# Retention and two feed-forward layers: decay tables for the queries, and another start order of weights and first steps

## The chip, the cores and the metric

One core of one Trainium2 chip. The metric is device time in microseconds (us), the median of three runs: 961.13 us before (960.35 to 962.30). Below, PE is TensorE, ACT is ScalarE, DVE is VectorE, POOL is GpSimd and SP is the queue that issues the transfers.

## What is computed

Four sequences of 576 positions, 8 heads of 64 columns. Attention without a softmax: the scores are scaled and multiplied by a decay, one gamma for each head. Its output (2304 tokens of 512) goes through two feed-forward layers, all in float32.

```python
gamma = 1.0 - 2.0 ** (-5.0 - np.arange(H))
Dmat = np.where(rel >= 0, gamma[:, None, None] ** rel[None, :, :], 0.0)
attn = np.matmul(scores * Dmat, v)              # scores = q k^T / sqrt(64)
h = x @ w_in                                    # x: 2304 x 512, w_in: 512 x 2048
x2 = (np.maximum(h, 0) + alpha * np.minimum(h, 0)) @ w_out
y = (sigmoid(x2 @ w_gate) * (x2 @ w_val)) @ w_out2   # d_ff 1536
```

## The kernel before, in words

The 2304 tokens are cut into blocks of 256, 512, 512, 512 and 512 (`BLOCKS`, line 27); block 0 is the short one. Attention goes by chunks of at most 128 positions (`CHUNKS`), 21 in all: two of block 0, five of block 1 (one of them of 64 positions, and another at its end), the rest of blocks 2 to 4.

Attention in chunks. For a chunk, q is multiplied by gamma to the power of the position inside the chunk and k (through v's rows) by its inverse, both on POOL (`att_q`, line 252, and `att_v`, line 260). PE makes the scores s (`att_scores`, line 267), DVE masks them, and PE makes o from the masked scores and v (`att_values`, line 285). What earlier chunks of the sequence give stands in a state `m_sb`, one 128x128 block for each pair of heads: PE multiplies it with q into o (line 294), then makes the chunk's own k-v product m (line 300), DVE adds it into the state (line 308, or copies it for a first chunk, line 310), and POOL multiplies the whole state by gamma to the power of the chunk's length (line 313), so that it fits the next chunk. The next chunk's product with the state waits for that. `split` (line 125) leaves the result as two float32r parts, the high one by ACT, the rest by DVE; the two parts of x and of each weight are multiplied in three products (`products`, line 384), which stand for one float32 product.

The weights come as raw words of 512 KB and are made into two such parts in `prepare_weight` (line 143): two ACT passes (lines 149 and 151), three DVE steps (155, 156, 159), one ACT pass (166) and one last DVE step (168). `begin_weight` starts one and issues the load of a further one; `weight_step(n)` (line 204) adds n to a credit, begins a weight whenever the credit reaches 1, and moves all that are under way by one step. `weight(...)` does so until a weight that is asked for is there. The first layer has 32 such blocks: key (1, f, 0) is a column block of w_in, (1, f, 1) a row block of w_out, f from 0 to 15.

`ffn1_h(j, f)` (line 393) makes hidden block f of token block j: 12 matmuls, then ACT and DVE apply the two slopes (lines 400 to 405), then the split into g. The two PSUM buffers of `ps_h` are free again after g's split on DVE (line 128). `ffn1_y(j, f)` (line 418) adds g times w_out's block into four output accumulators.

The order of PE's work is the program's own (a manual schedule). On the other engines a scheduler sets the order of the instructions when the program is built, and each engine's queue runs in that order. The program starts with `att_run` (line 349) over the seven chunks of blocks 0 and 1, whose argument `pace` says how fast weights are prepared beside it (`PACE_A`, `PACE_B`), and whose `fill` puts `EARLY` hidden blocks of token block 0 between the chunks, from chunk `LATE` on. Then a loop over f (line 501) makes the rest of block 0, with `BESIDE` = 11 of block 1's 16 steps beside it. The loop over token blocks 1 to 4 (line 519) has the attention of the block behind it as stages between its steps (`att_stages`, line 335), and prepares the second layer's weights in block 4; the second layer closes.

All weights, raw words, chunks (qk, kv) and g lie in one pool `big` of `NSLOT` = 39 slots of 4 KB a partition (line 92). A load waits until a slot is free.

Of the kernel before, what the change touches and what calls it, by code (L numbers as in the profile page):

```python
# [26 lines left out]
BLOCKS = (256, 512, 512, 512, 512)  # L27
FIRST = tuple(sum(BLOCKS[:j]) for j in range(len(BLOCKS)))
NBLK = len(BLOCKS)
NSLOT = 39  # L30

ORDER = (1, 2, 3, 4, 0)

NEXTRA = 1


EARLY, LATE = 5, 2

BESIDE = 11

# [2 lines left out]
BEHIND = 2  # L43


PACE_A, PACE_B, PACE_C, PACE_E, PACE_F = 0.55, 0.5, 0.7, 0.65, 1


def chunks():
# [12 lines left out]


CHUNKS = chunks()


LENGTHS = sorted({c[3] for c in CHUNKS})
O_M = NPAIR * P
O_GK = O_M + P
O_GP = O_GK + H  # L70
N_CST = O_GP + len(LENGTHS) * NPAIR


def constants():
    gamma = (1.0 - 2.0 ** (-5.0 - np.arange(H, dtype=np.float32))).astype(np.float64)
    i = np.arange(P)
    head = 2 * np.arange(NPAIR)[None, :] + (i // D)[:, None]
    out = np.zeros((P, N_CST), np.float32)
    out[:, :O_M] = (gamma[head][:, :, None] ** i / np.sqrt(D)).reshape(P, -1)
    out[:, O_M:O_GK] = i[None, :] >= i[:, None]  # L80
    out[:, O_GK:O_GP] = gamma ** -i[:, None]
    out[:, O_GP:] = (gamma[head][:, None, :] ** np.array(LENGTHS)[None, :, None]).reshape(P, -1)
    return out


# [1 line left out]
def retention_two_ffn(ctx: ExitStack, tc: tile.TileContext, att, cst, alpha, w1, w2, out):  # L87
# [85 lines left out]

    to_load = [(1, f, 0) for f in range(EARLY)]
    for f in range(NF1):
        to_load += [(1, f + EARLY, 0)] * (f + EARLY < NF1) + [(1, f, 1)]
    to_prepare = list(to_load)
    under_way = []

# [40 lines left out]
    def load_chunk(n):  # L220
        if n >= len(CHUNKS) or n in raw_a:
            return
        load_qk(n)
        load_kv(n)
# [27 lines left out]
    x_t = {}  # L252
    def att_q(n):

        c = CHUNKS[n][3]
        for part in (slice(0, 2), slice(2, 4)) if n == 0 else (slice(0, 4),):
            q = raw_a[n][0][:, 0, part, :c]
            nc.gpsimd.tensor_tensor(out=q, in0=q, in1=decay[:, part, :c], op=ALU.mult)  # L258

    def att_v(n):  # L260

        c = CHUNKS[n][3]
        v = raw_a[n][1][:c, 1, :].rearrange("p (h d) -> p h d", h=H)
        gk = c_sb[:c, O_GK:O_GP]
        nc.gpsimd.tensor_tensor(out=v, in0=v, in1=gk.unsqueeze(2).to_broadcast([c, H, D]), op=ALU.mult)

    def att_scores(n, pool, tags):
# [17 lines left out]
    def att_values(n, s_sb, pool, tags):  # L285

        j, _, pos, c, col = CHUNKS[n]
        qk, kv = raw_a[n]
        last = pos + c == S
        o_ps = pool.tile([P, NPAIR, P], F32, tag=tags[0], name=f"o{n}")  # L290

        if pos:
            for pr in range(NPAIR):
                nc.tensor.matmul(o_ps[:, pr, :c], m_sb[:, pr, :], qk[:, 0, pr, :c], start=pr == 0, stop=False)  # L294
        if not last:
            m_ps = pool.tile([P, NPAIR, D], F32, tag=tags[1], name=f"m{n}")
            for pr in range(NPAIR):
                for e in range(2):
                    h = 2 * pr + e
                    nc.tensor.matmul(  # L300
                        m_ps[e * D:(e + 1) * D, pr, :], kv[:c, 0, h * D:(h + 1) * D],
                        kv[:c, 1, h * D:(h + 1) * D], start=True, stop=True,
                    )
            for e in range(2):
                r = slice(e * D, (e + 1) * D)
                dst = m_sb[r, :, e * D:(e + 1) * D]
                if pos:
                    nc.vector.tensor_tensor(out=dst, in0=dst, in1=m_ps[r], op=ALU.add)
                else:
                    nc.vector.tensor_copy(dst, m_ps[r])  # L310
            g = O_GP + LENGTHS.index(c) * NPAIR
            g = c_sb[:, g:g + NPAIR].unsqueeze(2).to_broadcast([P, NPAIR, P])
            nc.gpsimd.tensor_tensor(out=m_sb, in0=m_sb, in1=g, op=ALU.mult)
        for pr in range(NPAIR):
            for e in range(2):
                h = 2 * pr + e
                nc.tensor.matmul(  # L317
                    o_ps[e * D:(e + 1) * D, pr, :c], kv[:c, 1, h * D:(h + 1) * D], s_sb[e][:c, pr, :c],
                    start=pos == 0 and pr == 0, stop=pr == NPAIR - 1,
                )  # L320
        x = x_t[j]
        split(x[:, 0, :, col:col + c], x[:, 1, :, col:col + c], o_ps[:, :, :c])
# [147 lines left out]
    nc.gpsimd.memset(m_sb, 0.0)  # L470
    load_chunk(0)
    load_chunk(1)
    load_weights(1)
    load_chunk(2)
    nc.sync.dma_start(out=al_sb, in_=alpha)
    nc.scalar.activation(na_sb, al_sb, AF.Copy, scale=-1.0)
    load_weights(2)
    load_chunk(3)
    load_weights(1)

    pa, py = (ps_a, "ab"), (ps_y, "yy")
    n0, n1 = len(runs_of(0)), len(runs_of(1))
# [14 lines left out]

    att_run(runs_of(0) + runs_of(1), [pa, py, py], lambda i: PACE_A if i < n0 else PACE_B, first_h, 4)

    step1 = 0  # L500
    for f in range(NF1):
        if done[0] < NF1:
            ffn1_h(0, done[0])
            done[0] += 1
            weight_step(PACE_C)
        ffn1_y(0, f)
        weight_step(PACE_C)
        if step1 * NF1 < BESIDE * (f + 1):
            ffn1_h(1, step1)
            weight_step(PACE_C)  # L510
            later(BEHIND - 1)
            weight_step(PACE_C)
            late.append((1, step1))
            step1 += 1
    n = runs_of(2)[0]
    load_chunk(n)
    att_q(n)
# [89 lines left out]
```

## Time and profile before

| | |
|---|---|
| Median of three runs | 961.13 us |
| The profiled execution | 963.9 us, its span 962.0 us |
| PE busy | 925.9 us, 96% of the span |
| PE weight loads | 777.5 us (beside PE) |
| DVE busy | 441.1 us, 46% |
| ACT busy | 288.8 us, 30% |
| POOL busy | 64.9 us, 7% |
| Moved by the transfers | 69.8 MB, 73 GB/s in the mean |

The span is the time from the first to the last instruction of one profiled execution. Busy times of different engines overlap. Shares of the whole span are means over stretches with different limits, so they are to be read with the views by stretch. A wait is idle time of an engine, put down to the instruction that ended it.

### The profile page before, as it was taken

How to read it: one execution, taken by the hardware profiler on the slowest of the kernel's cores; microseconds unless marked ns; L12 is line 12 of the kernel's file. 1: busy time of each engine (PE TensorE's matmuls, PEld its weight loads, DVE VectorE, ACT ScalarE, POOL GpSimd, SP SyncE). 2: the span in 40 equal slices, each digit the busy share in tenths (PEclk: the TensorE clock that was granted, in tenths of full speed). 3: DMA queues.
4: the chain of work that ended last, by engine and by line, in shares of the span. 5: the costliest groups of instructions: out<-in, count | busy, mean ns of one | idle time of the engine just before them, and what ended most of it. 6: DMA issues, size and time to landing. Idle time of an engine off the chain costs nothing.

```text
span 962.0 us, 12270 instructions
## 1 busy us (share of the span) xinstructions
PE 925.9 (96%) x5032; PEld 777.5 (81%) x5032; DVE 441.1 (46%) x730; ACT 288.8 (30%) x532; POOL 64.9 (7%) x62
## 2 busy tenths in 40 slices
PE   5777999999999999999999999999999999999998
PEld 4666998888888888887888888888888888888897
DVE  4999952545444544449877851221122112211212
ACT  2577820111011101137766641121112111211211
POOL 5410000131120111000000000000000000000000
PEclk9868999999999999999999999999999999999999
DMA  9932201332110310035552500100011000100100
GB/s 326 382 116 79 76 2 44 110 110 88 45 44 24 100 53 23 22 114 195 154 165 101 192 22 1 65 24 1 0 48 41 1 1 33 33 1 1 44 1 22
DMA packets 27975, 69.81 MB, mean 73 GB/s; under 512 B 6928, under 2 KB 8464, under 8 KB 27920
## 3 DMA queue, kind: packets, MB, share of 16 engines
q1 hardware_dynamic: 27920, 69.04, 21.2%
q8 instruction: 39, 0.64, 0.3%
q14 instruction: 16, 0.13, 0.0%
HBM read 59.59 MB, written 9.44 MB: 72 GB/s over the span
## 4 chain that ended last, share of the span: by engine, by line
PE 89%; DVE 7%; issue 1%; DMA 1%; ACT 1%; SPq 0%; DVEq 0%; ACTq 0%
PE z L388 31%; PE h L388 19%; PE y L388 18%; PE o L388 15%; DVE r L156 2%; DVE r L159 1%; PE s L275 1%; PE o L317 1%; DVE w L168 1%; PE o L294 1%; PE y0b L388 1%; PE y0a L388 1%; DMA r<-w 1%; DVE t L155 1%; PE m L300 1%
## 5 line engine op out<-in xcount | busy, mean ns | idle before, releaser
L388 PE MATMUL z<-x,w 128*128 128x512 f32 (+1 forms) x1440 | 305.3, 368 | 0.0
L388 PEld LDWEIGHTS z<-x,w 128*128 128x128 f32 x1440 | 252.4, 188 | 45.9
L388 PE MATMUL h<-x,w 128*128 128x512 f32 (+1 forms) x960 | 220.1, 380 | 11.6 <-DVE g L128 11.2
L388 PEld LDWEIGHTS h<-x,w 128*128 128x128 f32 x960 | 172.0, 195 | 46.3 <-DVE g L128 14.0
L388 PE MATMUL y<-g,w 128*128 128x512 f32 x768 | 187.5, 393 | 1.9 <-ACT yst L415 1.9
L388 PEld LDWEIGHTS y<-g,w 128*128 128x128 f32 x768 | 143.9, 189 | 33.7 <-ACT yst L415 2.3
L455 DVE TENSOR_TENSOR z<-sg,z 128x512 f32<-128x512 f32 (+1 forms) x60 | 38.6, 643 | 258.2 <-PE z L388 258.2
L388 PE MATMUL o<-w,p 128*128 128x512 f32 x648 | 156.8, 389 | 0.0
L388 PEld LDWEIGHTS o<-w,p 128*128 128x128 f32 x648 | 120.9, 188 | 24.6
L127 ACT ACTIVATE g<-h 128x512 fp32r<-128x512 f32 (+1 forms) x80 | 44.2, 553 | 232.7 <-DVE h L405 222.7
L404 DVE TENSOR_SCALAR t<-h,al_sb 128x512 f32<-128x512 f32 (+1 forms) x47 | 34.5, 734 | 113.2 <-PE h L388 113.2
L454 ACT ACTIVATE sg<-z 128x512 f32<-128x512 f32 (+1 forms) x60 | 33.3, 554 | 170.8 <-PE z L388 170.7
L127 ACT ACTIVATE p<-z 128x512 fp32r<-128x512 f32 (+1 forms) x60 | 33.4, 556 | 131.8 <-DVE z L455 131.8
L128 DVE TENSOR_TENSOR g<-h,g 128x512 fp32r<-128x512 f32 (+1 forms) x80 | 50.8, 634 | 25.6 <-ACT g L127 25.0
L128 DVE TENSOR_TENSOR p<-z,p 128x512 fp32r<-128x512 f32 (+1 forms) x60 | 38.2, 637 | 32.6 <-ACT p L127 32.5
L156 DVE CUSTOM_DVE_ANT_0 r<-r,t 128x1024 uint16<-128x1024 uint16 x68 | 49.3, 729 | 4.1 <-ACT r L151 0.2
L159 DVE SCALAR_TENSOR_TENSOR r<-r 128x512 uint32<-128x512 uint32 x68 | 49.9, 734 | 0.5
L149 ACT ACTIVATE r<-r 128x512 f32<-128x512 f32 x68 | 45.5, 669 | 12.0 <-DMA r<-w 12.0
L166 ACT ACTIVATE w<-r 128x512 fp32r<-128x512 f32 x68 | 44.0, 672 | 15.9 <-DVE r L159 14.8
L168 DVE TENSOR_TENSOR w<-r,w 128x512 fp32r<-128x512 f32 x68 | 46.3, 698 | 1.6 <-ACT w L166 1.5
L151 ACT ACTIVATE r<-r 128x512 int32<-128x512 uint32 x68 | 45.9, 675 | 0.0
L258 POOL TENSOR_TENSOR qk<-qk,c_sb 128x512 f32<-128x512 f32 (+1 forms) x21 | 25.0, 1193 | 160.1 <-DMA qk<-att 160.1
(45 smaller groups left out, 510.8 us busy)
## 6 DMA issues: line engine op xcount, KB each, us to landing
r<-w SPq DMA_DIRECT2D x68, 512.0 KB, 4.4
kv<-att SPq DMA_DIRECT2D x16, 512.0 KB, 4.1
qk<-att SPq DMA_DIRECT2D x15, 512.0 KB, 3.5
y<-ost SPq DMA_DIRECT2D x18, 256.0 KB, 2.0
x2d<-yst SPq DMA_DIRECT2D x16, 256.0 KB, 2.1
x2r<-x2d SPq DMA_DIRECT2D x16, 256.0 KB, 2.9
qk<-att SPq DMA_DIRECT2D x6, 256.0 KB, 3.7
kv<-att SPq DMA_DIRECT2D x4, 256.0 KB, 6.3
```

Source lines behind the costliest of these rows:

```text
L127: nc.scalar.activation(hi, src, AF.Copy)
L128: nc.vector.tensor_tensor(out=lo, in0=src, in1=hi.bitcast(F32), op=ALU.subtract)
L149: nc.scalar.activation(high.bitcast(F32), high.bitcast(F32), AF.Copy, scale=2.0 ** -112)
L151: nc.scalar.activation(low.bitcast(I32), low, AF.Copy, scale=2.0 ** -29)
L156: nc.vector.tensor_tensor(out=low.bitcast(I32), in0=low.bitcast(I32), in1=top.bitcast(I32), op=ALU.add)
L159: nc.vector.scalar_tensor_tensor(low, high, 0x80000000, low, ALU.bitwise_and, ALU.bitwise_or)
L166: nc.scalar.activation(w[:, 0, :], low.bitcast(F32), AF.Copy)
L168: nc.vector.tensor_tensor(out=w[:, 1, :], in0=low.bitcast(F32), in1=w[:, 0, :].bitcast(F32), op=ALU.subtract)
L388: nc.tensor.matmul(ps, l, r, start=first and i == 0, stop=last and i == len(todo) - 1)
L404: nc.vector.tensor_scalar(t, ps, 0.0, al_sb[:, f:f + 1], ALU.min, ALU.mult)
L454: nc.scalar.activation(t, ps[0], AF.Sigmoid)
L455: nc.vector.tensor_tensor(out=ps[1], in0=t, in1=ps[1], op=ALU.mult)
```

## The change

q's decay table of a chunk that isn't the first of its sequence is no longer the table of positions inside the chunk: ACT multiplies that table by gamma to the power of the chunk's start, in four pieces of up to 128 columns, into a tile `dec` of two buffers, and POOL multiplies q by it. v gets the inverse power of the position in the sequence. The state is then the plain sum of the chunks' products, and POOL's multiplication of it is gone. The constants hold the inverse powers and the factors for the five starts (748 columns where there were 656). The pool has 38 slots.

The start has another order as well. Loads: chunk 2 now comes ahead of the first weight, and chunk 3 ahead of the second. In the list of weights (1, f, 1) comes ahead of (1, f + EARLY, 0), and `EARLY` is 2 instead of 5. Fewer weights are prepared beside attention (`PACE_A` 0.08 for 0.55, `PACE_B` 0.14 for 0.5), two hidden blocks of block 0 stand between its chunks instead of five, and the loop over f takes block 1's step ahead of block 0's, with two of block 1's hidden blocks at its very start.

```diff
-NSLOT = 39
+NSLOT = 38
...
-EARLY, LATE = 5, 2
+EARLY, LATE = 2, 4
...
-PACE_A, PACE_B, PACE_C, PACE_E, PACE_F = 0.55, 0.5, 0.7, 0.65, 1
+PACE_A, PACE_B, PACE_C, PACE_E, PACE_F = 0.08, 0.14, 0.5, 0.65, 1
...
-        to_load += [(1, f + EARLY, 0)] * (f + EARLY < NF1) + [(1, f, 1)]
+        to_load += [(1, f, 1)] + [(1, f + EARLY, 0)] * (f + EARLY < NF1)
...
     def att_q(n):
 
-        c = CHUNKS[n][3]
+        _, _, pos, c, _ = CHUNKS[n]
+        by = decay
+        if pos:
+
+            by = ap.tile([P, NPAIR, P], F32, tag="dec", name=f"dec{n}", bufs=2)
+            for pr in range(NPAIR):
+                g = O_GP + STARTS.index(pos) * NPAIR + pr
+                nc.scalar.activation(by[:, pr, :c], decay[:, pr, :c], AF.Copy, scale=c_sb[:, g:g + 1])
         for part in (slice(0, 2), slice(2, 4)) if n == 0 else (slice(0, 4),):
             q = raw_a[n][0][:, 0, part, :c]
-            nc.gpsimd.tensor_tensor(out=q, in0=q, in1=decay[:, part, :c], op=ALU.mult)
+            nc.gpsimd.tensor_tensor(out=q, in0=q, in1=by[:, part, :c], op=ALU.mult)
...
                     nc.vector.tensor_copy(dst, m_ps[r])
-            g = O_GP + LENGTHS.index(c) * NPAIR
-            g = c_sb[:, g:g + NPAIR].unsqueeze(2).to_broadcast([P, NPAIR, P])
-            nc.gpsimd.tensor_tensor(out=m_sb, in0=m_sb, in1=g, op=ALU.mult)
...
     load_chunk(1)
+    load_chunk(2)
     load_weights(1)
-    load_chunk(2)
+    load_chunk(3)
     nc.sync.dma_start(out=al_sb, in_=alpha)
     nc.scalar.activation(na_sb, al_sb, AF.Copy, scale=-1.0)
     load_weights(2)
-    load_chunk(3)
-    load_weights(1)
...
+    load_weights(2)
     step1 = 0
     for f in range(NF1):
+
+        while step1 < EARLY or (step1 - EARLY) * (NF1 - 1) < (BESIDE - EARLY) * f:
+            ffn1_h(1, step1)
+            weight_step(PACE_C)
+            later(BEHIND - 1 if step1 >= EARLY else EARLY)
+            late.append((1, step1))
+            step1 += 1
+            if step1 > EARLY:
+                break
+        ffn1_y(0, f)
+        weight_step(PACE_C)
+        weight_step(PACE_C)
         if done[0] < NF1:
             ffn1_h(0, done[0])
             done[0] += 1
-            weight_step(PACE_C)
-        ffn1_y(0, f)
         weight_step(PACE_C)
-        if step1 * NF1 < BESIDE * (f + 1):
-            ffn1_h(1, step1)
-            weight_step(PACE_C)
-            later(BEHIND - 1)
-            weight_step(PACE_C)
-            late.append((1, step1))
-            step1 += 1
+        weight_step(PACE_C)
```

Where instructions move, first on PE, behind the attention of blocks 0 and 1. h and g carry the hidden block's number, x_124 and x_122 are block 0's input, x_200 and x_193 block 1's, y0a and y0b block 0's output and y_0 to y_3 block 1's. Before:

```order
L388 MATMUL h_4_623<-x_124,w_4_0_349 128x256 x12
L388 MATMUL h_5_654<-x_124,w_5_0_375 128x256 x12
L388 MATMUL y0a<-g_0_339,w_0_1_432 128x256 x6
L388 MATMUL y0b<-g_0_339,w_0_1_432 128x256 x6
L388 MATMUL h_0_702<-x_200,w_0_0_196 128x512 x12
L388 MATMUL h_6_738<-x_124,w_6_0_458 128x256 x12
L388 MATMUL y0a<-g_0_339,w_1_1_504 128x256 x6
L388 MATMUL y0b<-g_0_339,w_1_1_504 128x256 x6
L388 MATMUL h_1_783<-x_200,w_1_0_227 128x512 x12
```

Now:

```order
L395 MATMUL h_0_503<-x_193,w_0_0_313 128x512 x12
L395 MATMUL h_1_523<-x_193,w_1_0_405 128x512 x12
L395 MATMUL y0a<-g_0_398,w_0_1_496 128x256 x6
L395 MATMUL y0b<-g_0_398,w_0_1_496 128x256 x6
L395 MATMUL h_2_580<-x_122,w_2_0_567 128x256 x12
L395 MATMUL h_2_613<-x_193,w_2_0_567 128x512 x12
L395 MATMUL y_0_638<-g_0_520,w_0_1_496 128x512 x3
```

Behind attention the old order asks for the fifth and sixth column block of w_in and then adds block 1's first hidden block; the new one has two hidden blocks of block 1, whose weights are there already, and asks for the third column block after them.

The second place is the queue of DVE at the start of attention: sc and qk are a chunk's masks, t, r and w the steps of a weight (its number and its half behind the letter), m_sb the state's update, x a split of attention's output. Before:

```order
L279 TENSOR_TENSOR qk_99<-s_0_144,c_sb 128x512
L310 COPY m_sb<-m_168 64x4x64 x2
L168 TENSOR_TENSOR w_0_0_196<-r_0_0_103,w_0_0_196 128x512
L155 TENSOR_SCALAR t_1_0_221<-r_1_0_111 128x512
L156 ISA r_1_0_111<-r_1_0_111,t_1_0_221 128x512x2
L128 TENSOR_TENSOR x_124<-o_167,x_124 128x4x128
L159 SCALAR_TENSOR_TENSOR r_1_0_111<-r_1_0_111 128x512
L155 TENSOR_SCALAR t_2_0_259<-r_2_0_113 128x512
L156 ISA r_2_0_113<-r_2_0_113,t_2_0_259 128x512x2
L168 TENSOR_TENSOR w_1_0_227<-r_1_0_111,w_1_0_227 128x512
L159 SCALAR_TENSOR_TENSOR r_2_0_113<-r_2_0_113 128x512
L279 TENSOR_TENSOR sc_211<-s_1_202,c_sb 128x512
```

Now:

```order
L170 TENSOR_TENSOR w_0_0_313<-r_0_0_107,w_0_0_313 128x512
L157 TENSOR_SCALAR t_1_0_401<-r_1_0_115 128x512
L158 ISA r_1_0_115<-r_1_0_115,t_1_0_401 128x512x2
L289 TENSOR_TENSOR sc_204<-s_1_195,c_sb 128x512
L289 TENSOR_TENSOR qk_103<-s_0_194,c_sb 128x512
L157 TENSOR_SCALAR t_0_1_466<-r_0_1_117 128x512
L161 SCALAR_TENSOR_TENSOR r_1_0_115<-r_1_0_115 128x512
L158 ISA r_0_1_117<-r_0_1_117,t_0_1_466 128x512x2
L318 TENSOR_TENSOR m_sb<-m_sb,m_223 64x4x64 x2
L161 SCALAR_TENSOR_TENSOR r_0_1_117<-r_0_1_117 128x512
L130 TENSOR_TENSOR x_122<-o_218,x_122 128x4x128
L289 TENSOR_TENSOR sc_254<-s_1_245,c_sb 128x512
```

Fewer weight steps stand between the masks of chunk 2 (sc_204) and those of chunk 3 (sc_254), but some still stand in front of each.

The third place is the queue of transfers, SP, at its start. Before:

```order
L249 DMA kv_101<-att 128x1024
L138 DMA r_0_0_103<-w 128x1024
L239 DMA qk_105<-att 128x1024
L249 DMA kv_107<-att 128x1024
L475 DMA al_sb<-alpha 128x16
L138 DMA r_1_0_111<-w 128x1024
L138 DMA r_2_0_113<-w 128x1024
L239 DMA qk_115<-att 128x1024
L249 DMA kv_117<-att 128x1024
L138 DMA r_3_0_119<-w 128x1024
L239 DMA qk_140<-att 128x8x64
```

Now:

```order
L251 DMA kv_101<-att 128x1024
L241 DMA qk_103<-att 128x1024
L251 DMA kv_105<-att 128x1024
L140 DMA r_0_0_107<-w 128x1024
L241 DMA qk_109<-att 128x1024
L251 DMA kv_111<-att 128x1024
L483 DMA al_sb<-alpha 128x16
L140 DMA r_1_0_115<-w 128x1024
L140 DMA r_0_1_117<-w 128x1024
L241 DMA qk_143<-att 128x8x64
L251 DMA kv_145<-att 64x1024
```

Chunks 2, 3 and 4 come one weight, two weights and one weight earlier, and the third weight that is loaded is a block of w_out.

## Rows read from the trace of the kernel before

**Rows 1.** The page, slices of 24 us, busy tenths and granted clock.

```profile
PE   5777999999999999999999999999999999999998
PEclk9868999999999999999999999999999999999999
```

**Rows 2.** Windows: length, then busy us and count of PE, PEld, DVE, ACT, POOL; clock, DMA.

```profile
48.00:72.00 24.00, 17.15 (x139) 15.54 (x140) 23.83 (x48) 18.81 (x40) 2.49 (x2) 0.64 0.33 117
72.00:96.00 24.00, 18.65 (x87) 14.96 (x86) 23.59 (x46) 17.56 (x35) 0.00 (x0) 0.86 0.24 77
```

**Rows 3.** Waits of PE in the whole span: total us, times, longest.

```profile
PE h L388 <- DVE g L128: 11.2, 4, 3.1
PE o L294 <- POOL m_sb L313: 9.7, 3, 6.4
PE s L275 <- POOL qk L258: 9.3, 2, 5.6
```

**Rows 4.** The chain in order of time, behind 98 us: start us, us on it.

```profile
98.03 1.43 PE h L388 x12
99.46 0.72 PE y0a L388 x6
...
103.78 2.75 PE h L388 x12
106.53 2.72 PE y L388 x12
```

**Rows 5.** The same chain between 63 and 81 us, DVE's steps.

```profile
63.74 0.42 DVE x L128
...
71.63 0.40 DVE h L402
72.03 0.59 DVE r L159
72.63 0.34 DVE t L155
72.97 0.60 DVE r L156
73.57 0.60 DVE w L168
74.17 0.34 DVE g L128
...
77.58 0.67 DVE h L402
...
80.04 0.60 DVE g L128
```

**Rows 6.** Timeline of POOL, first chunks: start us, us; in brackets the idle time before.

```profile
9.00 1.04 POOL L265 TENSOR_TENSOR kv<-kv,c_sb 128x512 f32<-128x512 f32 x1 [2.40 <-DMA kv<-att]
...
14.67 1.54 POOL L258 TENSOR_TENSOR qk<-qk,c_sb 128x512 f32<-128x512 f32 x1 [2.17 <-DMA qk<-att]
```

**Rows 7.** Timeline of PE, two products with the state.

```profile
32.09 2.08 PE L294 MATMUL o<-qk,m_sb 128*128 128x128 f32 x8 [6.44 <-POOL m_sb L313]
...
39.32 1.16 PE L294 MATMUL o<-qk,m_sb 128*128 128x128 f32 x8
```

**Rows 8.** Timeline of DVE, beside POOL's work.

```profile
17.28 0.67 DVE L279 TENSOR_TENSOR qk<-s,c_sb 128x512 f32<-128x512 f32 x1
17.88 0.84 DVE L310 COPY m_sb<-m 64x256 f32<-64x256 f32 x2
...
20.76 1.53 DVE L156 CUSTOM_DVE_ANT_0 r<-r,t 128x1024 uint16<-128x1024 uint16 x1
```

**Rows 9.** Timeline of ACT, a pass of 16 and one of 512 columns.

```profile
17.37 0.21 ACT L476 ACTIVATE na_sb<-al_sb 128x16 f32<-128x16 f32 x1
...
74.53 0.60 ACT L400 ACTIVATE t<-h 128x512 f32<-128x512 f32 x1
```

**Rows 10.** Waits of SP from 130 to 420 us: total us, times, longest.

```profile
SPq L249 <- PE y L388: 79.2, 11, 14.3
```

More of the change, by code (lines that the diff above doesn't have):

```diff
@@ L64 @@
 CHUNKS = chunks()
-LENGTHS = sorted({c[3] for c in CHUNKS})
+STARTS = sorted({c[2] for c in CHUNKS})
+NST = len(STARTS)
 O_M = NPAIR * P
 O_GK = O_M + P
-O_GP = O_GK + H
-N_CST = O_GP + len(LENGTHS) * NPAIR
+O_GP = O_GK + NST * H
+N_CST = O_GP + NST * NPAIR
 def constants():
@@ L80, in constants @@
     out[:, O_M:O_GK] = i[None, :] >= i[:, None]
-    out[:, O_GK:O_GP] = gamma ** -i[:, None]
-    out[:, O_GP:] = (gamma[head][:, None, :] ** np.array(LENGTHS)[None, :, None]).reshape(P, -1)
+    st = np.array(STARTS)
+    out[:, O_GK:O_GP] = (gamma ** -(st[None, :, None] + i[:, None, None])).reshape(P, -1)
+    out[:, O_GP:] = (gamma[head][:, None, :] ** st[None, :, None]).reshape(P, -1)
     return out
@@ L253, in att_q @@
     def att_q(n):
-        c = CHUNKS[n][3]
+        _, _, pos, c, _ = CHUNKS[n]
[5 more added lines that the diff above has]
+                nc.scalar.activation(by[:, pr, :c], decay[:, pr, :c], AF.Copy, scale=c_sb[:, g:g + 1])
         for part in (slice(0, 2), slice(2, 4)) if n == 0 else (slice(0, 4),):
             q = raw_a[n][0][:, 0, part, :c]
-            nc.gpsimd.tensor_tensor(out=q, in0=q, in1=decay[:, part, :c], op=ALU.mult)
+            nc.gpsimd.tensor_tensor(out=q, in0=q, in1=by[:, part, :c], op=ALU.mult)
     def att_v(n):
-        c = CHUNKS[n][3]
+        _, _, pos, c, _ = CHUNKS[n]
+        st = O_GK + STARTS.index(pos) * H
         v = raw_a[n][1][:c, 1, :].rearrange("p (h d) -> p h d", h=H)
-        gk = c_sb[:c, O_GK:O_GP]
+        gk = c_sb[:c, st:st + H]
         nc.gpsimd.tensor_tensor(out=v, in0=v, in1=gk.unsqueeze(2).to_broadcast([c, H, D]), op=ALU.mult)
```

## The prediction

> **What bounds the kernel now.** I read the page's slices first, then the windows, then who makes TensorE (PE) wait, and last the chain. The slices [rows 1] show PE full from the fifth slice (24 us each) to the end, with holes and a clock below full only in the first four. The windows [rows 2] name the engine that is full while PE is not: VectorE (DVE), 23.83 of 24 us in 48 to 72 and 23.59 in the next, while PE has 17.15 and 18.65 at a mean clock of 0.64 and 0.86, that is partly at the lower of its two levels, 1.2 instead of 2.4 GHz. From 96 us PE is full. PE's waits [rows 3] say the same by name: 11.2 us for g, DVE's last step on a hidden block, 9.7 us for POOL's scaling of the state, 9.3 us for POOL's scaled q, all of it in the first 98 us. So only the first 98 us can give much, and DVE's in-order queue is what to follow there. Its load is the split of w1 into two parts: 32 blocks, each 0.34 + 0.60 + 0.60 + 0.60 = 2.14 us by the distance from start to start in the chain [rows 5], 68.5 us in all.
>
> **A sum that needs one unknown.** From 98.03 us PE is its own bound. Its matmul steps there cost 1.43 us (h of block 0), 2 x 0.72 (y of block 0), 2.75 (h of block 1) and 2.72 (y of block 1) [rows 4]. By PE's order the step at 98.03 is the ninth h of block 0; done by then are eight h and three y of block 0, three h and one y of block 1: 11.4 + 4.3 + 8.3 + 2.7 = 26.7 us of work. In the changed order I take the start of the third h of block 0 (h_2) as mark and call it X. Ahead of it stand two h and one y of block 0 and two h of block 1: 2.9 + 1.4 + 5.5 = 9.8 us. What PE does in total is the same, so the new span is X + (962.0 - 98.0) + 26.7 - 9.8 = **X + 880.9 us**, plus stalls behind X.
>
> **X, by DVE's queue.** Ahead of and with the last step of the weight that h_2 needs stand, in the new order: 14 masks (10 of 0.60 from start to start, 4 of 0.33 by their half width) 7.3; 12 half updates of the state at 0.40, 4.8 [rows 8]; 7 splits of x 3.7; four whole weights 8.6; the first three steps of four more, 6.2; two h+g of block 0 at 0.40 + 0.34 and two of block 1 at 0.67 + 0.60, 4.0 [rows 5]: 34.6 us. (In the old order DVE finished nine blocks of w1 ahead of attention's last x, in the new one three.) Nothing starts earlier than before: chunk 0's masks at 8 us, chunk 1's at 13.6. 33.4 us from 13.6 on, without any idle time, is 47.0: the lower bound of X, which gives 928 us of span. The upper bound is an attention as crowded as the old one: its last x was split at 64 us [rows 5], and h, h, y and the last weight after it take 7 us: X = 70, span 951.
>
> **Between the bounds** I walk the queues. Transfers: the four pieces of half a MB between the start on kv0 and that on qk2 took 14.67 - 9.00 us, 1.4 each [rows 6]; the last attention piece is now some 13 pieces behind kv0, 27.5 us, so data are no bound after 30. Waits: in the new order w1's second and third block stand in front of chunk 2's masks and chunk 1's state update on DVE, and wait for raw blocks that land at 20 and 21.6 us and two ScalarE (ACT) passes. PE reaches the o of chunk 2 at about 22 and gets its state at 26 to 27. After that gap I let PE run at the lower clock, as it did after the gap of 6.44 us in the trace (a group of eight with the state took 2.08 us, the next such group 1.16) [rows 7], to about 33. The next blocks in front (two raw blocks from 28.6 on, behind ACT's other work) hold chunk 4's state to 35 and chunk 5's masks to 39. Then two h, the last state and values: PE ends attention at 47, the last x is split at 49. Two h of block 1, 5.5 us, end at 54.5. The weight's last step stands behind both g on DVE: two ACT passes of 0.6 and a third [rows 9], h 0.67, g 0.60 and the weight's 0.60 [rows 5] put it at 58. **X = 58.4**.
>
> **A price inside this walk.** Where POOL is busy, DVE's steps are longer: the same L156 took 1.53 us at 20.76 and 0.60 later [rows 5, 8], while a mask, read from PSUM, kept its 0.60. Ten POOL multiplications of 1.0 to 1.5 us remain after 13.6 us. About eight weight steps fall among them: at 0.9 us each, at most 7 us, which the walk holds. If all forty steps of this stretch were stretched by 0.5 us, X would be 20 - 7 = 13 us later, 71, and the span 952. The Trainium skill (GPSIMD Engine Reference, Specifications) says that POOL contends with DVE instructions that read two SBUF inputs or run in a two-port mode. By that rule only the weight steps are hit, as these rows show, and the smaller price holds; without it the sum would be the larger one.
>
> **Behind X** I compare the sums of both queues. PE needs the weight of h_3 8.3 us after X, DVE has it 4.4 after; the y weight of f = 3: 18.1 against 16.2; h_7's: 30.8 against 29.1; h_9's: 47.4 against 40.4. So weights come in time, by 1 to 7 us. Twice a hidden PSUM buffer is late instead, because g stands behind weight steps: h of block 1 at f = 7 (51.8 against 52.6) and at f = 8 (61.6 against 65.1, less what PE has lost by then). DVE's sum to the last weight is 74 us behind X, PE's to the same place over 90. I take **3 us** of stalls; between 0 and the 11.2 us of the old order [rows 3].
>
> **Other edits.** The scaling of the state leaves POOL (17 times; the first six held PE for 9.7 us, gone, as the walk has it; the other eleven stand while PE is full, worth nothing). ACT makes 16 tables of four 128-column pieces: a piece lies between 0.21 us (16 columns) and 0.60 (512 columns) [rows 9], 0.30 on the line between them, 1.2 a table. Five are made for attention, in ACT's idle first 20 us; two more stand early in its queue and the first of them waits for POOL, holding an x split by a microsecond or two, in the walk. Nine fall beside a full PE, off its path: nothing. By the Trainium skill (ScalarE: Activation LUTs, What ACT_TABLE_LOAD costs) each pointer scale adds about 93 ns; an estimate by that page is 1.2 us a table, and the sum would be the same. Constants grow by 92 columns, under 0.2 us. One slot fewer: later loads already wait for slots, 79.2 us on kv alone [rows 10], yet PE did not wait; nothing, or the rival below.
>
> **Sum.** 58.4 + 880.9 + 3 = 942.3 span. The profiled execution took 963.9 with a span of 962.0, 1.9 around it, and lies 2.8 above the median of three runs, 961.1. So 942.3 + 1.9 - 2.8 = **941.4 us**.
>
> **Rivals.** *Attention at DVE's bound (0.14).* If raw blocks never hold DVE and the clock does not fall, X is 47 to 52, stalls 0 to 1: 928 to 934, say 931. For it: transfers now bring attention first. Against: the order puts weight steps in front of masks and state.
> *DVE still sets the pace (0.18).* The old trace's wait for g comes back [rows 3], 11 us in place of 3, or X is near 68: 950. For it: the sums lie within 1 to 3 us of each other up to f = 5, and where block 1 has no step, DVE needs 5.0 us for PE's 2.9. Against: pairs of steps balance.
> *Slots (0.05, slower).* With 38 slots, 32 weights and two or three g leave three or four for attention. Each of the 14 later chunks would have to wait for its neighbour's release, and PE for a transfer and a q of about 1.3 us (like those of [rows 6]). At 2.5 us each, 35 us: 976. It decides from 20 / 14 = 1.4 us a chunk. Against: PE did not wait once there, and a load has a whole step of 5.5 us to land.
> *No gain (0.03).* The order has another start but the same DVE work, and PE at the lower clock loses what the order wins: 961.
>
> **Numbers.** The forecast has 0.60, with its own range 934 to 949 (X by 6, stalls by 3). The range 931 to 954 leaves out half of the first rival, and the last two: 0.15 to 0.2. Faster 0.93, within 0.2% (1.9 us, about what a measurement can tell) 0.02, slower 0.05; the case without gain gives 0.02 to the second and 0.01 to the first of these.
>
> **What would show it.** Windows: PE full from about 58 us on, not 96; DVE full from 14 to some 130. PE's waits: none for POOL's state, a few us for g; the state's update on DVE in their place between 20 and 36. A PE wait behind 150 us would speak for the slots; DVE full with PE at 17 to 19 of 24 us past 60, for the second rival.

## The result, and the profile after

| | before | after |
|---|---|---|
| Median of four executions each | 961.38 us (960.35 to 962.30) | 951.44 us (951.14 to 952.36) |
| The profiled execution | 963.9 us, span 962.0 | 951.14 us, span 949.3 |
| PE busy | 925.9 us | 918.7 us |
| ACT busy | 288.8 us | 312.4 us |
| POOL busy | 64.9 us | 46.9 us |

The ratio is 0.9894, 95% interval 0.9879 to 0.9909: faster by 1.1%. The forecast was 941.4 us with a range of 931 to 954, so the time lies inside it, but 10 us above the forecast and 2.4 above the 934 to 949 that the prediction gave the forecast itself. These are the questions: what gave the 10 us of gain, and what took the 10 that I had expected on top?

The page of the changed kernel, slices of 23.7 us, answers to [rows 1]:

```profile
PE   4789899999999999999999999999999999999998
...
DVE  4969974555444544369787841221122112211212
...
PEclk9879999999999999999999999999999999999999
```

PE is at 8 or 9 tenths from the third slice on; before it was at 7 in the second, third and fourth. DVE is no longer full in the third slice: over a third of it is idle.

The windows, columns as in [rows 2]:

```profile
48.00:72.00 24.00, 21.48 (x92) 17.71 (x93) 15.16 (x28) 13.21 (x26) 0.00 (x0) 0.79 0.11 40
72.00:96.00 24.00, 23.61 (x151) 21.17 (x149) 22.70 (x44) 19.94 (x42) 0.00 (x0) 1.00 0.33 110
96.00:120.00 24.00, 21.61 (x128) 19.08 (x128) 23.86 (x47) 21.71 (x45) 0.00 (x0) 1.00 0.33 111
```

PE works 21.48 and 23.61 us where it worked 17.15 and 18.65 before. But the clock from 48 to 72 is 0.79 in the mean, and from 96 to 120, where PE was full, it now misses 2.4 us beside a full DVE.

PE's waits in the whole span, columns as in [rows 3]:

```profile
PE s L285 <- POOL qk L267: 8.0, 3, 5.5
PE o L304 <- DVE m_sb L318: 7.4, 1, 7.4
PE h L395 <- DVE g L130: 3.5, 3, 2.2
PE h L395 <- ACT w L168: 1.9, 2, 1.8
PE y L395 <- ACT yst L422: 1.9, 1, 1.9
PE h L395 <- ACT x L129: 1.7, 1, 1.7
PE h L395 <- DVE w L170: 1.5, 3, 1.0
```

The wait for POOL's scaling of the state, 9.7 us, is gone, and the 11.2 us for g have become 3.5. But in place of the former stands a single wait of 7.4 us for the state's update on DVE, so PE waits 2.3 us less for the state and not 9.7. The timeline of DVE shows what stands in front of that update (start us, us):

```profile
22.67 1.22 DVE L161 SCALAR_TENSOR_TENSOR r<-r 128x512 uint32<-128x512 uint32 x1
23.81 2.75 DVE L158 CUSTOM_DVE_ANT_0 r<-r,t 128x1024 uint16<-128x1024 uint16 x1
26.48 0.86 DVE L318 TENSOR_TENSOR m_sb<-m_sb,m 64x256 f32<-64x256 f32 x2
```

These two weight steps, the last ones in front, hold the state until 26.48, and both are stretched beside POOL: 2.75 us for the step that takes 0.60 elsewhere.

And the timeline of PE, with the idle time before each group in brackets (a group joins neighbours of one line, so x22 is the rest of h_2 of block 0 and the whole h_2 of block 1, and x23 is two h of block 1 but for a matmul):

```profile
27.49 2.05 PE L304 MATMUL o<-qk,m_sb 128*128 128x128 f32 x8 [7.37 <-DVE m_sb L318]
...
48.15 0.79 PE L395 MATMUL h<-x,w 128*128 128x512 f32 x1 [1.73 <-ACT x L129]
49.26 8.15 PE L395 MATMUL h<-x,w 128*128 128x512 f32 x23 [0.32 <-DVE x L130]
57.25 0.88 PE L395 MATMUL y0a<-g,w 128*128 128x256 f32 x6
...
60.63 0.50 PE L395 MATMUL h<-x,w 128*128 128x256 f32 x2 [1.78 <-ACT w L168]
61.40 5.76 PE L395 MATMUL h<-x,w 128*128 128x256 f32 x22 [0.27 <-DVE w L170]
...
118.38 4.30 PE L395 MATMUL h<-x,w 128*128 128x512 f32 x12 [2.18 <-DVE g L130]
122.47 3.27 PE L395 MATMUL y<-g,w 128*128 128x512 f32 x12
...
425.02 1.66 PE L395 MATMUL y<-g,w 128*128 128x512 f32 x6 [1.90 <-ACT yst L422]
```

The place that I called X, the start of h_2 of block 0, is at 60.63 us. The two h of block 1 ahead of it last from 48.15 to 57.25, 9.1 us, where [rows 4] had 2.75 for one. The short windows inside, with the granted clock as the third number from the end, say why:

```profile
50.00:54.00 4.00, 4.00 (x11) 3.13 (x10) 1.10 (x2) 0.00 (x0) 0.00 (x0) 0.50 0.00 0
62.00:66.00 4.00, 4.00 (x16) 3.48 (x16) 2.10 (x5) 2.29 (x6) 0.00 (x0) 0.60 0.00 0
120.00:122.00 2.00, 2.00 (x6) 1.56 (x5) 2.00 (x5) 0.31 (x1) 0.00 (x0) 0.50 0.00 0
```

PE is busy all the time in these windows, at 0.50, the lower of its two levels, in the first and the third, and at it for most of the second (0.60). Each stretch follows a wait of about 2 us: 1.73 and 0.32, 1.78 and 0.27, 2.18.

### The profile page after: what moved, and what is told of

It is laid out like the page before. It is cut to its first block, busy times and chain, and to the rows that moved or that the text cites. A ratio compares the mean times of both kernels' runs of the same rounds, so it can differ in the third digit from the quotient of the medians.

```text
span 949.3 us, 12323 instructions
## 1 busy us (share of the span) xinstructions
PE 918.7 (97%) x5032; PEld 770.8 (81%) x5032; DVE 433.6 (46%) x725; ACT 312.4 (33%) x606; POOL 46.9 (5%) x46
## 4 chain that ended last, share of the span: by engine, by line
PE 90%; DVE 5%; ACT 2%; issue 1%; DMA 1%; SPq 1%; POOL 0%; ACTq 0%; DVEq 0%; POOLq 0%
PE z L395 31%; PE h L395 20%; PE y L395 18%; PE o L395 16%; PE s L285 1%; PE o L304 1%; PE o L324 1%; DVE r L158 1%; DMA qk<-att 1%; PE m L310 1%; DVE r L161 1%; PE y0b L395 1%; PE y0a L395 1%; DVE w L170 1%; ACT r L151 1%
## 5 line engine op out<-in xcount | busy, mean ns | idle before, releaser
L411 DVE TENSOR_SCALAR t<-h,al_sb 128x512 f32<-128x512 f32 (+1 forms) x42 | 31.0, 738 | 97.0 <-PE h L395 97.0
L409 DVE SCALAR_TENSOR_TENSOR h<-h,na_sb,t 128x512 f32<-128x512 f32 (+1 forms) x38 | 25.0, 658 | 22.7 <-ACT h L408 22.7
```

Source lines behind the costliest of these rows:

```text
L411: nc.vector.tensor_scalar(t, ps, 0.0, al_sb[:, f:f + 1], ALU.min, ALU.mult)
```

## The experiments

My theory after the result: the order and the tables do what the forecast says, and what is missing is TensorE's clock behind short waits, which I had charged to the long wait in attention alone. The rivals: the time lies in DVE's steps in front of the state; or DVE's queue sets the pace behind attention, so that whatever PE gains earlier it gives back later. The last two columns give the mean granted clock of the executions (lowest to highest) and what it can have cost at most, in the median: one minus the clock, times the span. It costs less where PE waits in such a stretch anyway.

| kernel | median us (lowest to highest) | ratio to before, 95% interval | clock | at most, us |
|---|---|---|---|---|
| before (in e1's comparison) | 962.22 (958.94 to 964.19) | 1 | 0.979 to 0.988 | 17.3 |
| changed kernel | 951.44 (951.14 to 952.36) | 0.9894 (0.9879 to 0.9909) | 0.987 to 0.989 | 10.5 |
| e1 gaps filled | 947.91 (945.94 to 948.47) | 0.9853 (0.9826 to 0.9879) | 0.993 to 0.996 | 5.7 |
| e2 new order alone | 958.95 (954.22 to 961.19) | 0.9966 (0.9945 to 0.9986) | 0.982 to 0.991 | 13.4 |
| e3 tables alone | 958.01 (956.41 to 962.19) | 0.9967 (0.9949 to 0.9985) | 0.982 to 0.991 | 13.4 |
| e4 slots alone | 961.24 (960.02 to 962.93) | 0.9995 (0.9982 to 1.0008) | 0.979 to 0.986 | 15.3 |
| e5 filled attention | 953.75 (953.67 to 954.90) | 0.9912 (0.9897 to 0.9927) | 0.993 | 6.7 |
| e6 weights later | 948.70 (948.40 to 950.35) | 0.9862 (0.9845 to 0.9878) | 0.989 to 0.993 | 7.6 |
| e7 slower weights | 954.79 (953.00 to 956.47) | 0.9920 (0.9905 to 0.9935) | 0.986 to 0.989 | 12.4 |
| e8 = e6 and e1 | 945.61 (944.98 to 948.31) | 0.9830 (0.9815 to 0.9845) | 0.995 to 0.996 | 3.8 |
| e9 = e8, weights last | 944.99 (944.84 to 947.81) | 0.9831 (0.9812 to 0.9851) | 0.995 to 0.998 | 3.8 |
| e10 = e8, two paces | 945.38 (944.76 to 946.00) | 0.9831 (0.9814 to 0.9847) | 0.995 to 0.998 | 3.8 |
| e11 = e8, late y | 943.20 (942.26 to 944.91) | 0.9801 (0.9778 to 0.9825) | 0.996 to 0.998 | 2.8 |
| e12 late y alone | 949.33 (947.59 to 951.17) | 0.9857 (0.9830 to 0.9883) | 0.989 to 0.993 | 8.1 |

The last column taken from the first leaves 940 to 943 us for the changed kernel and for e1 and e6 to e12. So most of what separates these kernels can be the clock. The column is a bound, and a coarse one: for before, it leaves 942 to 949 us in the four comparisons that these runs come from.

**e1: the two gaps filled.** Matmuls whose result is overwritten at once stand ahead of the first h of block 1 and of h_2 of block 0, so that PE is busy where it waited.

```diff
+WARM = {(1, 0): 16, (0, 2): 16}
...
+        for _ in range(WARM.get((j, f), 0)):
+            nc.tensor.matmul(ps[:, :256], wt[1, 0, 0][:, 0, :P], x_t[0][:, 0, 0], start=True, stop=True)
         products(ps, [(cols(w, k), x_t[j][:, :, k]) for k in range(KC)])
```

> The changed kernel with 16 matmuls of 256 columns more ahead of two hidden steps (the first of block 1, the third of block 0), into the PSUM tile that the step then begins anew, so that PE works through two gaps of some 2 us; their product is thrown away. Theory (the forecast was missed by PE's lower clock behind short gaps: two hidden blocks of block 1 took 9.1 us from 48.15 on where 5.5 were counted, the next two 2 us more than counted): the clock stays at its upper level there, 3.3 + 1.9 us come back, 946 to 947 us against 951.4. Rival (the order of DVE's queue sets the pace and the clock only fills what PE would wait anyway): 951, within 1 us.

Measured: 947.91, 3.5 us below the changed kernel; the rival (951) did not hold. PE's timeline in e1:

```profile
50.05 5.51 PE L397 MATMUL h<-x,w 128*128 128x512 f32 x23 [0.51 <-DVE x L132]
...
59.54 4.21 PE L397 MATMUL h<-x,w 128*128 128x256 f32 x22 [0.27 <-DVE w L172]
...
115.28 3.01 PE L397 MATMUL h<-x,w 128*128 128x512 f32 x12 [2.16 <-DVE g L132]
...
420.75 2.32 PE L397 MATMUL y<-g,w 128*128 128x512 f32 x6 [1.88 <-ACT yst L426]
```

The same 23 matmuls take 5.51 us instead of 8.15, the 22 take 4.21 instead of 5.76, though PE does more work and waits just as long for the same data. That shows the clock's share, 2.6 + 1.55 us at these two places. The other profiles of the new start with the tables or without say the same: with the gaps filled (e1, e8 to e11) the 23 matmuls took 5.49 to 5.55 us, without it 7.92 to 8.38, and 6.88 in e6; the 22 took 4.20 or 4.21 in e1, e8, e10 and e11, and without filling 5.76 to 5.78, and 4.21 in e6. Two things I had not expected. The wait for g at 115 us is as long as before, 2.16 us, but the h behind it takes 3.01 us, not 4.30: this time the clock stayed. And the wait for yst, 1.88 us, has a y of 2.32 us behind it, where the changed kernel had 1.66. The windows around it, of e1 and of the changed kernel:

```profile
420.00:424.00 4.00, 3.25 (x9) 2.60 (x10) 4.00 (x8) 3.29 (x7) 0.00 (x0) 0.69 0.44 172
```

```profile
425.00:429.00 4.00, 3.98 (x17) 3.30 (x18) 4.00 (x8) 3.00 (x5) 0.00 (x0) 1.00 0.58 190
```

So behind waits of 1.9 to 2.2 us the clock falls in one execution and not in another. e1's profile was 4.27 us ahead of the changed kernel's before this place (420.75 against 425.02) and 2.6 at the end (spans 946.7 and 949.3): 1.7 us were lost behind that one wait.

**e2 and e3: order and tables apart.** e2 has the new order and 38 slots, with v's inverse powers and POOL's scaling of the state as before; e3 has the tables and 38 slots, with every line on the order as before. The core of the difference, from the changed kernel to e2:

```diff
-            for pr in range(NPAIR):
-                g = O_GP + STARTS.index(pos) * NPAIR + pr
-                nc.scalar.activation(by[:, pr, :c], decay[:, pr, :c], AF.Copy, scale=c_sb[:, g:g + 1])
...
+            nc.gpsimd.tensor_tensor(out=m_sb, in0=m_sb, in1=g, op=ALU.mult)
```

and to e3:

```diff
-EARLY, LATE = 2, 4
+EARLY, LATE = 5, 2
...
-PACE_A, PACE_B, PACE_C, PACE_E, PACE_F = 0.08, 0.14, 0.5, 0.65, 1
+PACE_A, PACE_B, PACE_C, PACE_E, PACE_F = 0.55, 0.5, 0.7, 0.65, 1
```

> The changed kernel with the old decay: no tables, the state multiplied on POOL after each chunk; the new start order and 38 slots stay. Theory (the order carries most of the gain): 954 to 957 us, the state's way over POOL coming back at 1.0 to 1.5 us for each of four or five chunks, all before 50 us. Rival (the tables carry the gain): 960 to 962.

> The changed kernel with the old start order: loads, list of weights, paces, loop over f as before; tables, unscaled state and 38 slots stay. Theory (DVE's queue bounds the old start, so PE's 9.7 us of waits for POOL's scaling turn into waits for DVE): 958 to 961 us, within 3 us of before. Rival (that wait lay on the path): 951 to 953.

Measured: 958.95 and 958.01. e2 lies between its theory (954 to 957) and its rival (960 to 962), so the order does not carry most of the gain; e3 came out at its theory's lower end. Alone, each is worth 0.3%; together they are worth 1.1%, more than the sum (by the ratios 3.3 and 3.2 us against 10.2). PE's waits, e2 first, then e3:

```profile
PE o L292 <- POOL m_sb L311: 9.3, 3, 7.6
...
PE h L386 <- DVE g L126: 3.5, 4, 2.1
```

```profile
PE h L395 <- DVE g L130: 10.2, 5, 3.6
...
PE o L304 <- DVE m_sb L318: 7.1, 1, 7.1
```

With the order alone the wait for g has fallen from 11.2 to 3.5 us, but the state still passes through POOL and holds attention for 9.3 us; block 1's first h starts at 52.9 us instead of 48.15. With the tables alone the state waits for DVE instead, 8.5 us in two places, and attention hands on sooner (its last k-v product starts at 55.45 us, before at 57.78). But g's 10.2 us are still there: DVE, full (23.57 of 24 us from 48 to 72), takes the gain back. Each part leaves one of the two waits of [rows 3] nearly as it was, and that one then ends last. The executions of both lie wide apart (e2: 954 to 961), so the size of each is known to some 2 us only.

**e4: the slots.** The kernel before with `NSLOT = 38`.

```diff
-NSLOT = 39
+NSLOT = 38
```

> The kernel before with 38 slots in place of 39, nothing else. Theory (loads that wait for slots are hidden beside a full PE): 961 us, within 1 us of before. Rival (the slot paid for the tables costs time, which the rest of the change pays back): 964 or more.

Measured: 961.24, ratio 0.9995 (0.9982 to 1.0008). The slot costs nothing that shows. In its profile, as in that of the changed kernel, the only wait of PE behind 150 us is the 1.9 us for yst.

**e5: the wait in attention filled.** Seven float32 products of no use stand in front of chunk 2's product with the state.

```diff
+WAIT = {2: 7}
...
+        for _ in range(WAIT.get(n, 0)):
+            nc.tensor.matmul(o_ps[:, :, :], kv[:c, 0, :P], kv[:c, 0, :], start=True, stop=True)
```

> The changed kernel with seven matmuls of 512 float32 columns more, ahead of chunk 2's product with the state, where PE waits 7.4 us for DVE's state update; they use that chunk's k rows and write the PSUM tile that the product then begins anew. Theory (the lower clock behind a gap costs as well as the gap): the wait itself stays, but the group behind it takes 1.16 us instead of 2.05, m 0.69 instead of 1.12, the values 1.0 instead of 1.7: 2 us, 949 to 950. Rival (DVE's queue alone sets the end of this attention): 951 to 952.

Measured: 953.75, slower than the theory and the rival had it. The clock did what the theory says; PE's timeline in e5 has 1.05 us for the group that took 2.05:

```profile
28.19 1.05 PE L308 MATMUL o<-qk,m_sb 128*128 128x128 f32 x8
```

But this group starts at 28.19 where it started at 27.49, since the filling lasted longer than the wait, and DVE's order moved, too. DVE's timeline in e5:

```profile
30.07 0.43 DVE L159 TENSOR_SCALAR t<-r 128x512 uint32<-128x512 uint32 x1 [0.59 <-ACT r L153]
...
33.27 0.69 DVE L163 SCALAR_TENSOR_TENSOR r<-r 128x512 uint32<-128x512 uint32 x1
```

Six weight steps, from 30.07 to 33.9, now stand in front of the next chunk's state, and PE waits 3.5 us for that one; block 1's first h starts at 50.70 us instead of 48.15. So this run does not give the worth of the clock there in time; it shows that room in front of the state is filled with weight steps.

**e6: weights loaded later.** Two weights less are loaded at the start; they are loaded behind attention.

```diff
-    load_weights(2)
...
-    load_weights(2)
+    load_weights(4)
```

> The changed kernel with one weight loaded ahead instead of three, the other two after attention: chunk 2's masks and state update then stand in DVE's queue ahead of the second and third weight's steps. Theory (those steps hold the update, so PE waits 7.4 us from 20 on): the wait falls to 2 or 3 us, attention ends 4 to 5 us earlier, 946 to 947 us. Rival (the transfers of chunks 4 to 6, or POOL, stand right behind): 949 to 951.

Measured: 948.70, a gain of 2.7 us, between the theory (946 to 947) and its rival (949 to 951), and not by the theory's mechanism. DVE's timeline in e6:

```profile
21.45 0.86 DVE L318 TENSOR_TENSOR m_sb<-m_sb,m 64x256 f32<-64x256 f32 x2
...
27.81 0.43 DVE L157 TENSOR_SCALAR t<-r 128x512 uint32<-128x512 uint32 x1 [3.58 <-ACT r L151]
28.15 0.86 DVE L318 TENSOR_TENSOR m_sb<-m_sb,m 64x256 f32<-64x256 f32 x2
```

The update that came at 26.48 comes at 21.45. But the next one, at 28.15, stands behind a weight step that waits 3.58 us for ACT, and PE's wait of 7.4 us became two, 2.3 and 3.5. What held ACT is a decay table of the change itself, ahead of the weight's pass in ACT's queue; ACT's timeline in e6:

```profile
25.96 1.28 ACT L264 ACTIVATE dec<-c_sb 128x128 f32<-128x128 f32 x4 [4.38 <-POOL qk L267]
```

The table waits for POOL's q, the weight's pass starts behind it at 27.14, and the state's update stands behind that weight on DVE. Waits of 3.6 to 4.5 us of this table stand at the same place in e8 to e11. No run moved it, so what it costs is not shown. Attention ends hardly earlier; PE's timeline in e6:

```profile
49.34 6.88 PE L395 MATMUL h<-x,w 128*128 128x512 f32 x23 [1.04 <-DVE x L130]
...
60.20 4.21 PE L395 MATMUL h<-x,w 128*128 128x256 f32 x22 [0.27 <-DVE w L170]
```

The 23 matmuls start at 49.34 where they started at 49.26. They take 6.88 us instead of 8.15, and the 22 take 4.21 instead of 5.76: 2.8 us, all of it the clock; why it fell for less time here, with nothing filled, is not shown. The rival that the time lies in DVE's steps in front of the state is not decided by this run: taken from one update, the wait goes to the next, in front of which a weight step stands again.

**e7: a slower pace behind attention**, 0.45 for 0.5, to free g.

```diff
-PACE_A, PACE_B, PACE_C, PACE_E, PACE_F = 0.08, 0.14, 0.5, 0.65, 1
+PACE_A, PACE_B, PACE_C, PACE_E, PACE_F = 0.08, 0.14, 0.45, 0.65, 1
```

> The changed kernel with a pace of 0.45 instead of 0.5 weights a step beside the hidden blocks. Theory (g stands behind weight steps on DVE; the two waits of 2.2 and 1.1 us past 115 us and the lower clock behind the first are theirs): 947 to 949. Rival (weights then come late): 952 to 956.

Measured: 954.79; the rival held. PE's waits in e7:

```profile
PE h L395 <- ACT w L168: 4.6, 4, 1.8
PE h L395 <- DVE w L170: 3.2, 4, 1.0
...
PE h L395 <- DVE g L130: 1.4, 2, 1.0
```

g's wait falls from 3.5 to 1.4 us and the weights' rises from 3.4 to 7.8. The weights have no room to be later; a faster pace was not run.

**e8: e6 and e1 together**, with 14 matmuls at each place for 16.

> The later weights and the two filled gaps of some 2 us behind attention, together (14 matmuls each). Theory (the two losses are separate): the gains add, 942 to 944 us. Rival (an earlier attention only makes the waits behind it longer, filled or not): 946 to 948, as the filled gaps alone.

Measured: 945.61, 5.8 us below the changed kernel; the two gains of 2.7 and 3.5 would add to 6.2. So they nearly add, though the time lies between the theory's 942 to 944 and the rival's 946 to 948. By the table's last column the gain is the clock's again: 3.8 us at most are lost to it, against 10.5. In its profile the clock still fell behind the yst wait, as in e1.

**e9 and e10: more of the same?** e9 is e8 with `PACE_B` 0.06 for 0.14, e10 is e8 with this pace in the loop over f:

```diff
+SLOW, PACE_D = 4, 0.42
...
+        pace = PACE_C if f < SLOW else PACE_D
```

> The kernel of e8 with PACE_B 0.06 for 0.14: in DVE's order no weight step but one now stands ahead of the state's update of chunk 2, and none ahead of that of chunk 3; the weight steps come behind attention instead. If those steps are what attention still waits for (e8: 4.5 us of PE waits for the state, and the lower clock behind them), the waits fall below 2 us, attention ends 2 to 3 us earlier and the time is 942 to 944. Rival: what is taken out of attention comes back behind it, since DVE's queue is full from there to 130 us: waits for w and g grow by as much, 945 to 948.

> The kernel of e8 with a pace of 0.42 instead of 0.5 from the fifth round (f = 4) of the loop on. The waits for g in e8 (4.1 us, at f = 7 and f = 8) come, by the theory, from weight steps that stand in front of g while the weights are ahead of need; e7 slowed the pace from the start, where the weights have no lead. If so, the waits for g fall to about 1.5 us and none for weights come in their place: 942 to 944. Rival: the weights have no lead there either, PE waits for w instead: 946 to 950.

Measured: 944.99 and 945.38, both as e8, above both theories (942 to 944). In e9 both rows of waits move as the rival says: the state's falls from 4.5 to 3.6 us, g's rises from 4.1 to 4.6 and in more places. Its windows:

```profile
48.00:72.00 24.00, 22.78 (x128) 19.72 (x127) 23.68 (x46) 21.86 (x43) 0.00 (x0) 1.00 0.22 79
72.00:96.00 24.00, 23.04 (x146) 20.82 (x145) 23.81 (x47) 21.07 (x44) 0.00 (x0) 1.00 0.30 102
```

DVE is full from 48 us on (21.46 of 24 in e8's first of these windows). But attention did not end sooner in this profile: the 23 matmuls start at 47.16 us, in e8 at 46.95, and one weight step, which waits 2.91 us for ACT, still stands in front of the state's update at 28.01. So what an earlier end would give is not shown. In e10 g's wait fell as the theory says, from 4.1 to 2.6 us, without new waits for weights, but the 23 matmuls of block 1 start at 49.44 us in its profile against 46.95 in e8's, with the same program up to there: attention's end differs by that much from execution to execution, and the time does not show the 1.5 us.

**e11 and e12: the wait at 425 us.** The y of block 4's first hidden block comes one step later, on top of e8 (e11) and alone (e12).

```diff
-                    later(BEHIND - 1)
+                    later(BEHIND - 1 + ((j, f) == (NBLK - 1, 2)))
```

> The kernel of e8, and the first y step of block 4 comes one hidden block later, so that ScalarE has emptied block 3's accumulators by then. In e8 PE waited there 1.9 us, and the granted clock behind that wait was 0.67 and 0.91 for 8 us, some 1.7 us of work. By the theory that a wait of 1.9 us can cost as much again by the clock, the run gains about 3.6 us: 942. Rival (the wait alone counts, the clock costs nothing of its own): 1.9 us, 943.7. If ScalarE empties them later as well, nothing changes: 945.6.

> The changed kernel with the same one edit. In its profile the same wait of 1.9 us was followed by a clock of 1.00. So by the theory only the wait goes: 949.5. If its timed executions have the lower clock behind it, about 948; if the accumulators are emptied later as well, 951.4.

Measured: 943.20, 2.4 us below e8, and 949.33, 2.1 below the changed kernel. These are differences between comparisons in which before itself lay 0.2 to 1.1 us apart. The wait of 1.9 us is gone in both; PE's timeline in e11 now reads there:

```profile
415.79 3.02 PE L397 MATMUL h<-x,w 128*128 128x512 f32 x12 [0.16 <-DVE g L132]
418.64 5.60 PE L397 MATMUL y<-g,w 128*128 128x512 f32 x24
```

e12 is where the theory has it by its median (949.5), though its executions go from 947.6 to 951.2. e11 lies between the theory (942) and its rival (943.7), nearer to the rival, so the medians don't settle what the clock costs at this place; what it costs when it falls, 1.7 us, rests on e1's trace. One more row of e12's PE timeline belongs to the clock:

```profile
119.90 3.02 PE L395 MATMUL h<-x,w 128*128 128x512 f32 x12 [2.14 <-DVE g L130]
```

Up to here e12 is the changed kernel, and the wait is the same (2.14 against 2.18 us), yet the h behind it takes 3.02 us instead of 4.30. e11 is the fastest of all, 18 us below before in the same comparison (961.19).

## Why the prediction was right, and where it was 10 us off

**What bounds the kernel** was read rightly: all of the gain but 1.6 us (the tail, below) lies in the first 98 us, and e2 and e3 show that of the waits for g and for the state each holds the kernel when only the other is worked on. But less waiting is not all that it came from. Between the two profiled executions the span fell by 12.7 us. PE's idle time gives 5.5 of them (36.1 to 30.6); the other 7.2 are its busy time for the same 5032 matmuls (925.9 to 918.7). The mean clock went from 0.980 to 0.989, worth 8.8 us at most, so the likely cause of the 7.2 is that PE, waiting less often, ran more of its work at the higher level. The prediction does not name this part; it is in its sum because nearly all steps of the new start are priced at the higher level.

**X.** Predicted 58.4, measured 60.63. The walk had the state at 26 to 27 (27.5), the end of attention at 47 and the x split at 49 (the first h started at 48.15), and a wait of 2.5 us for the weight's last step behind both g (1.78). What failed is one term: "Two h of block 1, 5.5 us". They took 9.1, of which some 3 us are the lower clock, as e1 shows by the same matmuls. The walk charged that clock to the long gap in attention alone; here a wait of 1.73 us, one matmul and another 0.32 us were enough. The place itself differs between executions: in e12's profile, the same program up to there, X is at 62.11.

**Behind X.** The sum X + 880.9 holds for the work: from X to the yst wait PE needed 364.4 us, against 338.1 from 98.03 to the same place before [rows 4] plus the 16.9 us of steps that moved (26.7 - 9.8), 355.0. So 9.4 us of stalls, not 3: this is the second term that failed. Waits are 4.2 of them (PE's idle time from 60.63 to 132.62), and they stand where the prediction put them, g at f = 7 and f = 8, 2.18 and 1.12 us. The clock is 3.2: 5.76 us for 4.21, 4.30 for 3.02, 3.27 for 2.88. The last 2 us I can't put down to rows. Against this, the tail behind the yst wait was 1.6 us shorter than before. There the kernel before had, in its profiled execution, the lower clock (before, PE's timeline and a window):

```profile
436.14 2.44 PE L388 MATMUL y<-g,w 128*128 128x512 f32 x6 [1.90 <-ACT yst L415]
```

```profile
436.00:440.00 4.00, 3.86 (x10) 3.09 (x11) 4.00 (x9) 3.11 (x6) 0.00 (x0) 0.59 0.46 152
```

Together: + 2.2 for X, + 6.4 for the stalls, - 1.6 for the tail, 7.0 us between the predicted span of 942.3 and 949.3.

**From span to median.** I took off 2.8 us because the profiled execution of before lay that much above its median. That correction belongs to before alone: 1.6 us of it are, by the two traces, the clock behind one wait, which the changed kernel's profiled execution did not have (951.14, its median 951.44); where the other 1.2 come from no trace shows. The remaining 3 us of the miss are this step.

**The price beside POOL.** Right in kind: masks kept their 0.60 us, weight steps were stretched. One of them took 2.75 us, more than the 1.53 of [rows 8]; it stood in front of the state and is in the 7.4 us. The case that all forty steps are stretched did not come: up to X four are (1.64, 1.22, 2.75 and 1.21 us in DVE's timeline), not eight, by some 4 us in all, and from 48 to 120 us POOL has no work in the windows above.

**Tables, slots.** ACT's rows for two tables together and for one:

```profile
3.93 2.45 ACT L264 ACTIVATE dec<-c_sb 128x128 f32<-128x128 f32 x8 [1.91 <-DMA c_sb<-cst]
...
10.42 1.28 ACT L264 ACTIVATE dec<-c_sb 128x128 f32<-128x128 f32 x4 [4.05 <-POOL qk L267]
```

That is 1.2 to 1.3 us a table, as estimated; beside a full PE they cost nothing, since behind 150 us PE's only wait is that for yst. In attention one of them holds ACT's queue for some 4 us, which the walk had as a microsecond or two; in the changed kernel no wait of PE or DVE there is put down to it, in e6 the state's is. The slots cost nothing (e4). Some counts ahead of the result are off, and no term of the forecast hangs on them: there are 20 chunks with nine different starts, not 21 and five, and so 16 scalings of the state and 13 later chunks.

**The rivals.** The measured time is next to that of "DVE still sets the pace" (950), but not by its mechanism: PE waited 3.5 us for g in place of 11, and DVE was idle for 8.8 of the 24 us from 48 to 72, since PE, at the lower clock, was late with the h on which DVE's queue stood. So the sign "DVE full from 14 to 130" failed, and PE was not quite full past 58. In e9, where the clock is at 1.00 and attention shorter, DVE is full from 48 us on and PE waits for g in six places: there the rival's mechanism is back. Attention at DVE's bound, the slots and the case without gain are ruled out by the windows, e4 and the interval.

## What to carry to other kernels

Where two waits alternate on one engine's path, price their removal together: alone, each was worth a third of what both gave. A matmul step behind a wait of about 2 us is to be priced with the lower clock as the bad end of its range, even when such waits are short and few: the three here cost as much again as they lasted (6.2 us for 6.3). And before the distance from a profiled execution to the median is carried over to a changed kernel, look for what that one execution had that the others need not have.

## What the runs showed of the hardware that was not expected

The granted clock fell to 0.50 behind waits as short as 1.7 to 2.2 us between stretches of full work, and not every time. The wait for yst, 1.85 to 1.91 us in all profiles up to e10, had a clock of 1.00 behind it in the changed kernel and in e2 to e7 and e10, and of 0.59 to 0.73 over four us in before, e1, e8 and e9. The wait for g at f = 7, 2.1 to 2.2 us, was followed by an h of 4.3 to 4.5 us in the changed kernel, e2, e5 and e6, and of 3.0 in e12, where the program is the changed kernel's up to there, and in e1, e8 and e11. In e7's profile two pairs of waits of 1.33 and 0.95 us for a weight have 5.76 us for 22 matmuls behind the first (86.28) and 4.21 behind the second (101.86). Behind e8's wait of 1.61 us for g it did not fall. The executions of one program differ in the same way: the seven of before beside e11 took 960.6 to 961.2 us at clocks of 0.988 (and one 0.980), and 963.8 to 964.3 at 0.979 and 0.980. The Trainium skill (TensorE: Matmul & The Clock Gate, Part 1) says of the ramp at a kernel's start that the number of slow matmuls differs from run to run, and that its penalty is under 1% of a typical span and should not be fitted to a particular number of slow matmuls. The rows here show the same difference between executions behind short waits in the middle of a kernel. Their size, about 6 us of 949 outside attention, is 0.7%; but it is more than half of the whole gain, and most of the miss.

Filling such a wait with matmuls whose result is dropped removed the fall at the two places where it was done (e1, e8 to e11), and gained where the filling ended about when the data came. In e5 it outlasted them and came with another order on DVE, and the kernel was slower.
